# Moving attention work two to three steps sooner inside a feed-forward pipeline, with key-value products further ahead and one copy on another engine

## The chip, the cores and the metric

The kernel runs on one core of one Trainium2 chip. The metric is device microseconds of one execution. A profiled execution also gives a span, which is some 2 us below the time of the same execution. Verdicts use several timed executions of both kernels on the same chip.

## The reference, cut to what matters

Cosine-weighted linear attention over 8 batches of 576 tokens feeds a multiplicative feed-forward block over 4608 tokens:

```python
q_p, k_p = phi(q, cos_w, sin_w), phi(k, cos_w, sin_w)   # relu(x)*cos, relu(x)*sin: 128 features
kv  = einsum('bhsf,bhsd->bhfd', k_p, v)                 # key-value products
num = einsum('bhsf,bhfd->bhsd', q_p, kv)                # numerators
den = einsum('bhsf,bhf->bhs', q_p, sum(k_p)) + 1e-06
x   = num / den                                         # 4608 x 512
out = ((x @ w1) * (x @ w2)) @ w3 @ w_out
```

## The kernel before: the parts that the change and the argument touch

The feed-forward part runs in 9 tiles of 512 tokens. It is a generator that yields after each step, and attention work of later batches is put into the steps by hand. Tile t > 0 starts at step 40+24(t-1); in its first 16 steps it makes a and b products, with one ScalarE copy and one VectorE product for every two steps, and in its last 8 steps the output.

```python
def plan(b, kf, vc, kv, qf, nu, loads=None, xt=None):
    # kf/qf: features of k and q (VectorE half, ScalarE half; q then goes through a DMA transpose to qpT)
    # vc: value copies (GpSimd from batch 2 on); kv: key-value products; nu: numerators; xt: x transposes
    ...
        at(nu[i], lambda c=c: num(b, c))
        at(xt[i] if xt else nu[i], lambda c=c: x_tr(b, c))

def kv_chunk(b, c, i):
    ...                                       # 8 matmuls into pnum
    if i == NCH - 1:                          # after the fifth chunk
        nc.scalar.copy(out=kvs[:, 0:4, :], in_=kvt[:, 0, 0:260])
        nc.vector.tensor_copy(out=kvs[:, 4:8, :], in_=kvt[:, 1, 0:260])

def num(b, c, chain=True):
    nt = ps_att.tile([P, 2, 512], FP32, name="pnum")   # one buffer
    ...                                       # 8 matmuls, then den, reciprocal, xblk on VectorE

def x_tr(b, c, by_vector=False):
    if b >= 2 or (b == 1 and c == 3):
        nc.sync.dma_start_transpose(out=xT[t][:, :, ds(o, R)], in_=xf[rows])
        return
    ...                                       # 4 TensorE transposes into pst
    copy = nc.vector.tensor_copy if by_vector else nc.scalar.copy
    copy(out=xT[t][:, :, ds(o, R)], in_=pst[:, 0:4, rows])
...
bases = [74, 101, 125, 151, 175]              # step of the first numerator of batches 3 to 7
```

In the profiles, kvs is the copy of the key-value products, xblk a normalized block of x, qpT and xT the transposed q features and x, abT the feed-forward product, osb the copied output; pnum, pst and ffnps are PSUM tiles.

## Time and profile before

| | before |
|---|---|
| time, median of 3 (range) | 256.51 us (255.91 to 257.51) |
| time and span of the profiled execution | 258.77 us, 256.8 us |
| TensorE busy | 240.4 us (94%) |
| VectorE, ScalarE, GpSimd busy | 54%, 51%, 37% |
| holes of TensorE past 62 us, each over 0.1 us | 5.5 us |

TensorE's work is fixed, so everything turns on its holes, the stretches in which it stands idle. The profiled execution was itself 2 us slower than the median of the timed ones, which matters later. Its chain of waits, summed by engine (the page's part 4), is a first sign that some holes come from transfers:

```profile
PE 65%; DMA 23%; ACT 5%; issue 2%; DVE 2%; POOL 2%; ACTq 0%; POOLq 0%
```

Past 50 us the same chain, in order of time, has three DMA pieces: the q load of batch 2, the transpose of q at 146.36 that the prediction shows, and an x transpose (columns: start, us, what):

```profile
55.48 9.91 DMA qs<-in_q_dram
...
180.84 5.96 DMA xT<-xblk
```

### The profile page before, as it was taken

The page shows a single profiled execution, that of the slowest core. Times are in us where ns is not written, and L with a number is a line of the kernel's source. Part 1 is how long each engine was busy: PE and PEld are TensorE (multiplying, and loading weights), DVE is VectorE, ACT ScalarE, POOL GpSimd, SP SyncE. Part 2 cuts the span into 40 slices and gives each one's busy share as a digit, 9 for nine tenths or more (in the row PEclk, how much of TensorE's full clock was granted, in tenths as well). Part 3 has the DMA queues.
Part 4 walks back from the last instruction along what each step waited for, and adds up shares of the span by engine and source line. Part 5 has one row for each costly group of instructions (what it writes and reads, how often), then busy time and mean ns, then how long its engine had stood idle before and what let it go on. Part 6 is the DMA issues. An engine that isn't in the chain of part 4 may idle for free.

```text
span 256.8 us, 5008 instructions
## 1 busy us (share of the span) xinstructions
PE 240.4 (94%) x1837; PEld 130.6 (51%) x1867; DVE 138.6 (54%) x330; ACT 130.9 (51%) x270; POOL 94.2 (37%) x197
## 2 busy tenths in 40 slices
PE   8789999999789999999999997899999999999993
PEld 3478554565665445444544453345444544444442
DVE  6775654646668545646566654565567645312320
ACT  2675315667833683466446734474466433433322
POOL 7665140322232344125222711265125108886000
PEclk9999999999999999999999999999999999999999
DMA  6999999799999999999989999999999637998015
GB/s 191 182 194 203 208 205 203 92 127 166 138 157 116 174 155 151 130 127 210 165 119 143 208 118 163 138 178 135 184 151 172 126 72 138 327 289 270 2 39 124
DMA packets 83895, 41.02 MB, mean 160 GB/s; under 512 B 51488, under 2 KB 80416, under 8 KB 83872
## 3 DMA queue, kind: packets, MB, share of 16 engines
q0 software_dynamic: 35456, 27.20, 68.9%
q1 hardware_dynamic: 48256, 13.38, 33.5%
q8 instruction: 14, 0.23, 0.4%
q10 hardware_dynamic: 160, 0.13, 0.2%
q14 instruction: 9, 0.07, 0.1%
HBM read 38.80 MB, written 9.44 MB: 188 GB/s over the span
## 4 chain that ended last, share of the span: by engine, by line
PE 65%; DMA 23%; ACT 5%; issue 2%; DVE 2%; POOL 2%; ACTq 0%; POOLq 0%
PE ffnps L432 37%; PE ffnps L486 18%; DMA qs<-in_q_dram 7%; DMA w3b<-in_moe_w_dram 6%; DMA qpT<-qp 4%; DMA w2b<-in_moe_w_dram 3%; PE pnum L349 3%; PE ffnps L226 3%; DMA xT<-xblk 2%; PE pnum L291 2%; ACT qp L263 2%; DVE kvs L297 1%; PE pst L214 1%; ACT kvs L296 1%; DVE xblk L361 1%
## 5 line engine op out<-in xcount | busy, mean ns | idle before, releaser
L432 PE MATMUL ffnps<-xT,w1b 128*128 128x512 bf16 (+2 forms) x326 | 74.1, 347 | 2.7 <-ACT xT L389 1.1
L432 PE MATMUL ffnps<-xT,w2b 128*128 128x512 bf16 (+2 forms) x329 | 74.6, 348 | 0.4
L473 DVE TENSOR_TENSOR abT<-asb,ffnps 128x512 bf16<-128x512 bf16 x64 | 43.8, 685 | 44.1 <-PE ffnps L432 41.8
L469 ACT CAST asb<-ffnps 128x512 bf16<-128x512 f32 x64 | 37.4, 584 | 55.3 <-PE ffnps L432 48.9
L486 PE MATMUL ffnps<-w34b,abT 128*128 128x512 bf16 x270 | 63.3, 379 | 0.5
L521 POOL COPY seen<-mark 1x1 bf16<-1x1 bf16 x52 | 10.2, 195 | 99.1 <-ACT mark L519 99.1
L432 PEld LDWEIGHTS <-w1b 128*128 128x128 bf16 x336 | 30.7, 98 | 30.2 <-issue 2.8
L432 PEld LDWEIGHTS <-w2b 128*128 128x128 bf16 x336 | 30.3, 98 | 25.7
L486 PEld LDWEIGHTS <-abT 128*128 128x128 bf16 x280 | 26.0, 98 | 27.9 <-DVE abT L473 0.2
L493 ACT COPY osb<-ffnps 128x512 f32<-128x512 f32 x35 | 20.5, 585 | 38.1 <-PE ffnps L486 34.8
L263 ACT ACTIVATE qp<-qs,sinv 128x512 bf16<-128x512 bf16 (+2 forms) x40 | 28.1, 716 | 2.4 <-DMA qs<-in_q_dram 2.4
L361 DVE TENSOR_TENSOR xblk<-pnum,den 128x512 bf16<-128x512 f32 (+1 forms) x39 | 26.9, 691 | 1.4
L263 ACT ACTIVATE kp<-ks,sinv 128x512 bf16<-128x512 bf16 (+1 forms) x35 | 25.0, 720 | 2.3 <-DMA ks<-in_k_dram 2.3
L417 POOL DMA_DIRECT2D out_dram<-osb x42 | 22.2, 534 | 3.8 <-issue 2.8
L283 POOL COPY va<-vs 128x512 bf16<-128x512 bf16 (+1 forms) x30 | 17.7, 624 | 13.3 <-DMA vs<-in_v_dram 11.1
L349 PEld LDWEIGHTS <-qpT 128*128 128x128 bf16 x320 | 15.0, 98 | 12.1 <-issue 4.1
L259 DVE TENSOR_SCALAR qp<-qs,cosv 128x512 bf16<-128x512 bf16 (+1 forms) x40 | 19.2, 491 | 2.7 <-DMA qs<-in_q_dram 2.5
L359 DVE TENSOR_SCALAR den<-pnum 128x8 f32<-128x8 f32 (+1 forms) x39 | 6.4, 164 | 26.0 <-PE pnum L349 25.9
L349 PE MATMUL pnum<-kvs,qpT 128*128 128x65 bf16 x312 | 16.4, 194 | 2.7 <-DMA qpT<-qp 1.4
L226 PE MATMUL ffnps<-woutb,w3T 128*128 128x512 bf16 x62 | 14.8, 379 | 0.1
L291 PEld LDWEIGHTS <-kp 128*128 128x128 bf16 x280 | 11.5, 98 | 5.3 <-PE ffnps L432 1.3
L259 DVE TENSOR_SCALAR kp<-ks,cosv 128x512 bf16<-128x512 bf16 (+1 forms) x35 | 11.7, 343 | 4.1 <-DMA ks<-in_k_dram 4.1
(83 smaller groups left out, 179.9 us busy)
## 6 DMA issues: line engine op xcount, KB each, us to landing
out_dram<-osb POOLq DMA_DIRECT2D x16, 256.0 KB, 4.6
out_dram<-osb POOLq DMA_DIRECT2D x24, 128.0 KB, 3.8
qs<-in_q_dram POOLq DMA_DIRECT2D x9, 256.0 KB, 6.0
ks<-in_k_dram POOLq DMA_DIRECT2D x7, 320.0 KB, 5.8
qs<-in_q_dram POOLq DMA_DIRECT2D x7, 320.0 KB, 6.8
vs<-in_v_dram POOLq DMA_DIRECT2D x7, 320.0 KB, 5.2
ks<-in_k_dram POOLq DMA_DIRECT2D x7, 256.0 KB, 6.6
vs<-in_v_dram POOLq DMA_DIRECT2D x7, 256.0 KB, 5.0
```

Source lines behind the costliest of these rows:

```text
L226: nc.tensor.matmul(acc[:, :], lhsT=w3T[:, lc, :], rhs=woutb[:, lc, :], start=(lc == 0), stop=(lc == 7))
L259: nc.vector.tensor_scalar(out=dst[:R, c, :, 0:D], in0=src[:R, :, c, :], scalar1=0.0, scalar2=cosv[:R, at:at + 1], op0=ALU.max, op1=ALU.mult)
L263: nc.scalar.activation(out=dst[:R, c, 0:n, D:F], in_=src[:R, 0:n, c, :], func=ACTF.Relu, scale=sinv[:R, at:at + 1], bias=0.0)
L283: eng.tensor_copy(out=feat_of(b)[2][:R, c, :, 0:D], in_=raw[b, "v"][:R, :, c, :])
L349: nc.tensor.matmul(nt[:, h // 4, ds((h % 4) * 65, 65)], lhsT=qpT[:, h, ds(at, 128)], rhs=kvs[:, h, :], start=True, stop=True)
L361: nc.vector.tensor_tensor(out=xblk[rows], in0=n4[:, :, :, 0:D], in1=den[rows].unsqueeze(3).to_broadcast([R, 2, 4, D]), op=ALU.mult)
L417: on.dma_start(out=rows[:, :, cols], in_=osb[64 * i:64 * i + rows.shape[0], :, cols])
L432: nc.tensor.matmul(out, lhsT=w[:, kc, ts(jc, 128)], rhs=x[:, kc, tok], start=(kc == 0), stop=(kc == 3))
L469: nc.scalar.copy(out=asb[:], in_=aT[:, :])
L473: nc.vector.tensor_mul(out=abT[:, jc, :], in0=asb[:], in1=bT[:, :])
L486: nc.tensor.matmul(ops[:, :], lhsT=abT[:, jc, ts(ms, 128)], rhs=w34b[:, jc, :], start=(jc == 0), stop=(jc == 7))
L493: nc.scalar.copy(out=osb[:, ms % 2, :], in_=ops[:, :])
```

## The change

The intent is to give the transfers and evictions behind the attention part more steps before TensorE needs them. It has three parts, called (a), (b) and (c) throughout: (a) value copies and key-value products of batches 4 to 7 a step further ahead, (b) batch 1 and 2 around the start of tile 1, (c) the bases, with loads and stores.

```diff
-            at(xt[i] if xt else nu[i], lambda c=c: x_tr(b, c))
+            at(xt[i] if xt else nu[i], lambda c=c: x_tr(b, c, by_vector=(b, c) == (1, 1)))     # (b)
 plan(1, ...
-         ... nu=(35, 37, 38, 40, 43), xt=(37, 38, 40, 42, 43))
+         ... nu=(35, 37, 38, 40, 42), xt=(37, 38, 40, 41, 42))                                  # (b)
 plan(2, ...
-         kv=(45, 46, 46, 47, 47), qf=(40, 41, 42, 43, 44), ...
+         kv=(46, 46, 46, 47, 47), qf=(41, 42, 43, 44, 45), ...                                  # (b)
-    bases = [74, 101, 125, 151, 175]
+    bases = [74, 99, 123, 148, 173]                                                             # (c)
-        plan_loads(b, [last + s for s in (-8, -5, 1, 4, 8, 11)])
+        plan_loads(b, [last + s for s in (-8, -5, 1, 4, 7, 10)])                                # (c)
-             vc=[base + s for s in (-8, -7, -6, -5, -4)],
-             kv=[base + s for s in (-3, -2, -2, -2, -1)],
+             vc=[base + s for s in (-9, -8, -7, -6, -5)],                                       # (a)
+             kv=[base + s for s in (-4, -3, -3, -2, -2)],                                       # (a)
-        at((88, 115, 140, 166)[i] ...
+        at((88, 113, 137, 162)[i] ...                                                           # (c), stores
```

More of the change, by code (lines that the diff above doesn't have):

```diff
@@ L587 @@
     plan(1, kf=(22, 23, 24, 25, 26), vc=(31, 31, 32, 32, 32), kv=(33, 33, 33, 34, 34),
-         qf=(29, 30, 30, 31, 31), nu=(35, 37, 38, 40, 43), xt=(37, 38, 40, 42, 43))
+         qf=(29, 30, 30, 31, 31), nu=(35, 37, 38, 40, 42), xt=(37, 38, 40, 41, 42))
     for c, s in zip(order_of(1), (31, 32, 34)):
@@ L591 @@
     plan_loads(2, (27, 28, 31, 33, 35, 36))
-    plan(2, kf=(33, 35, 37, 39, 40), vc=(41, 42, 43, 44, 45), kv=(45, 46, 46, 47, 47),
-         qf=(40, 41, 42, 43, 44), nu=(48, 50, 52, 54, 57))
+    plan(2, kf=(33, 35, 37, 39, 40), vc=(41, 42, 43, 44, 45), kv=(46, 46, 46, 47, 47),
+         qf=(41, 42, 43, 44, 45), nu=(48, 50, 52, 54, 57))
     plan_loads(3, (46, 49, 53, 55, 58, 61))
@@ L610, in put @@
             store(nc.gpsimd, kept[i][:, :, :], 2 * i, 2)
-        at((88, 115, 140, 166)[i] if i < 4 else 185 + 2 * (i - 4), put)
+        at((88, 113, 137, 162)[i] if i < 4 else 185 + 2 * (i - 4), put)
     g = 0
```

## The prediction

> **What bounds the kernel now.** I read the page's header, engine row and slices first: is one engine busy nearly all the time, and at a full clock?
>
> ```profile
> span 256.8 us, 5008 instructions
> PE 240.4 (94%) x1837; PEld 130.6 (51%) x1867; DVE 138.6 (54%) x330; ACT 130.9 (51%) x270; POOL 94.2 (37%) x197
> PE   8789999999789999999999997899999999999993
> PEclk9999999999999999999999999999999999999999
> ```
>
> TensorE is busy for 240.4 of 256.8 us at full clock; no other engine passes 54%. The change removes no matmul, so it can only fill TensorE's 16.4 us of holes. About 8 us of these are the start (zeros, first k, first q, before 22 us) and the end (the last output copy and store, 4.3 us after the last matmul), which the change does not touch. So I asked for TensorE's own waits:
>
> ```profile
> PE pnum L349 <- DMA qpT<-qp: 1.4, 1, 1.4
> ...
> PE pnum L349 <- DVE kvs L297: 1.2, 4, 0.3
> PE ffnps L432 <- ACT xT L389: 1.1, 1, 1.1
> PE pnum L291 <- DVE xblk L361: 1.0, 1, 1.0
> PE ffnps L432 <- ACT osb L493: 0.8, 1, 0.8
> ```
>
> The columns are total us, times, longest. These five rows sum to 5.5 us (1.36 + 1.20 + 1.12 + 1.04 + 0.80 = 5.52) and are all the holes past 62 us above 0.1 us. They bound what the change can win: 2.1% of the time. The timeline of TensorE places them:
>
> ```profile
> 68.42 1.03 PE L432 MATMUL ffnps<-xT,w1b 128*128 128x256 bf16 x8 [1.12 <-ACT xT L389]
> ...
> 71.37 0.41 PE L291 MATMUL pnum<-va,kp 128*128 128x65 bf16 x8 [1.04 <-DVE xblk L361]
> ...
> 127.20 0.42 PE L349 MATMUL pnum<-kvs,qpT 128*128 128x65 bf16 x8 [0.30 <-DVE kvs L297]
> ...
> 157.07 0.43 PE L349 MATMUL pnum<-kvs,qpT 128*128 128x65 bf16 x8 [1.36 <-DMA qpT<-qp]
> ...
> 162.88 1.02 PE L432 MATMUL ffnps<-xT,w1b 128*128 128x512 bf16 x4 [0.80 <-ACT osb L493]
> ```
>
> Steps to time: tile t of the feed-forward part starts at step 40+24(t-1). Tile 1 (step 40) starts at 62.68 us, tile 5 (136) at 162.88. One step is four matmuls of 512 columns, 0.86 us apart on the timeline; attention work is put in between steps.
>
> The last row's label is wrong. The copy of osb it names is ScalarE's, but tile 5's first matmul needs batch 5's first 192 tokens, and the second of their two transposes was issued on the DMA queue at 156.72 and took 6.1 us to land, that is at 162.8, right before 162.88. It is a late DMA, not a PSUM buffer.
>
> **What the Trainium skill says.** "PSUM — Partial Sum Buffer", section "Engine vs sequencer instructions": the ScalarE, VectorE and GpSimd queues are strict FIFO, and matmuls start in program order. So one late input stops all work behind it; the trace agrees (a 1.12 us hole for one 0.57 us copy). "VectorE: DVE Perf Modes", section on the TRN2 errata: a copy out of PSUM costs ScalarE 172 + columns cycles at 1.2 GHz, 570 ns for 512 columns, and VectorE 120 + columns/2 at 0.96 GHz in a doubled mode, 392 ns. The trace has 580 and 425 ns for the x copy, so I use these. "DMA: Bandwidth & Descriptors", section "Issuing engines are not separate DMA queues": transfers from all engines run on the same 16 DMA engines and interleave. The trace agrees: the transposes of q for batch 5 beside a 512 KB store and two loads of k took a median of 9.0 us and at most 10.7, those of batch 7 with less beside them 3.2.
>
> **The change part by part.**
>
> (a) Key-value products a step further ahead, batches 4 to 7. Now the last of five chunks stands at base-1 and the first numerator at base. Between them TensorE has one step, 0.86 us, while two evictions in a row must finish (ScalarE 376 ns, VectorE 429 ns), with ScalarE first ending an asb copy. Around 125 to 127 us the last product ends at about 126.0, ScalarE starts kvs at 126.30, VectorE ends at 127.15, the numerator starts at 127.20. At base-2 there is a second step of 0.86 us, more than the hole of 0.30. I take all four: -1.2 us. Value copies also move one step, so the GpSimd copies stay ahead.
>
> (b) Batch 1 into tile 1. Tile 1's second half needs x of chunk 2, copied by ScalarE behind several activations:
>
> ```profile
> 67.18 0.72 ACT L263 ACTIVATE qp<-qs,sinv 128x512 bf16<-128x512 bf16 x1
> ...
> 67.81 0.57 ACT L389 COPY xT<-pst 128x512 bf16<-128x512 bf16 x1
> ```
>
> The change gives ScalarE one copy less (580 ns at 63.99), moves this transpose from step 42 to 41, the q features of batch 2 one step later, and batch 1's last numerator from 43 to 42. The instruction order confirms it: ScalarE now has kp (64 rows), asb, then xT. But there is a price. VectorE's 425 ns copy goes ahead of chunk 2's normalization:
>
> ```profile
> 64.24 0.17 DVE L359 TENSOR_SCALAR den<-pnum 128x8 f32<-128x8 f32 x1 [0.83 <-PE pnum L349]
> 64.44 0.20 DVE L360 RECIPROCAL den<-den 128x8 f32<-128x8 f32 x1
> 64.68 0.69 DVE L361 TENSOR_TENSOR xblk<-pnum,den 128x512 bf16<-128x512 f32 x1
> ```
>
> The copy runs 63.99 to 64.42, den starts about 64.45 instead of 64.24, xblk ends about 65.58 instead of 65.37. TensorE comes to that transpose at 64.91 now, not 65.78, and waits until about 65.63: a new hole of 0.7 us. Then xT is ready at about 66.6, while the second half is reached two half-tile groups later, near 67.9: the 1.12 hole goes. Batch 2's products move from 45 to 46 and the numerator before them from 43 to 42, four steps apart in place of two, so their wait for xblk (1.04) goes too. Sum: -1.12 - 1.04 + 0.72 = -1.44 us.
>
> (c) Batches 4 to 7 sooner. Numerators run at base, base+2, and so on; bases 101, 125, 151, 175 become 99, 123, 148, 173. Tile 5 starts at step 136, so batch 5's second transpose has 11 steps (125 to 136) in place of 9 (127 to 136): 1.73 us more for a landing 0.8 us late. -0.8 us.
>
> (d) The wait at 157.07 is not addressed as such. The chain has its cause:
>
> ```profile
> 146.36 10.67 DMA qpT<-qp
> ```
>
> This transpose belongs to q features at base-6 and serves the numerator at base+5; the distance is 11 steps before and after, the loads of the next batch keep base-8 and base-5, and the store keeps base-10. So if the transfers pile up likewise, 1.36 us stays; if that was a chance of this execution, it goes. I take half: -0.7 us.
>
> Sum: -1.2 - 1.44 - 0.8 - 0.7 = -4.1 us at the profile. I give back 0.3 for new small waits and 0.5 since the three timed runs (255.91 to 257.51) need not have every DMA delay of the profiled one, so there may be less to win. 256.5 - 3.3 = 253.2 us, 1.3% less.
>
> **The rivals.** First, v arrives too late. For batch 4 the load's second half moves from 85 to 84 but its first product from 98 to 95, 13 steps down to 11; batch 5 keeps 10, batch 6 goes from 12 to 11, batch 7 from 10 to 11. Loads of v land in about 5 us, 6 steps, and the copies take 0.62 us each. Batch 7 lived with 10 steps without a hole, so I give a new wait 15%; it would be about 1 us per batch, 255 to 256 us in all.
>
> Second, VectorE becomes the bound: with numerators at 99, 101 and 123, 125 more of them fall in a tile's first 16 steps, where two steps (1.73 us) hold a product (0.69), a normalization (1.1) and q features (0.35 to 0.5), 2.1 to 2.3 us. Against: batch 4 had this already at 101 and 103, and TensorE had no hole at 129. Four PSUM buffers take up a lag of two steps. If it binds, 0.5 us a batch: 254.5 us.
>
> Third, the DMA pile-up moves instead of going: the wait of 1.36 us may come again in batch 5, 6 (transposes already took 7.0 us median there) or both: 254 to 255 us.
>
> Fourth, everything goes and (d) too, without the hole of (b): 251.0 to 251.5 us, the best case.
>
> **Range and chances.** Between (a) + half of (b), about 254.8, and all of it less the new hole, 251.7: the range is 252.0 to 255.0. Faster by over 2% means below 251.4, practically all 5.5 us: 6%. Slower by 2% needs 5 us of new waits, which no view suggests: 1%. Within 2%: 93%.
>
> **What would show it.** (a) No row of TensorE waiting for kvs, from four. (b) The hole before the first-half-to-second-half matmul and the one before batch 2's products gone, and one of about 0.7 us before an x transpose near 65.6. (c) No hole at tile 5's start. (d) Either the qpT row gone or still 1 to 1.5 us. PE busy stays at 240 us. The prediction is wrong if GpSimd's value copies or late loads appear as TensorE's releasers, if DMA rows grow over 2 us, or if the timed kernel keeps its time while these rows vanish from the profile: then the profile's holes were not the timed runs' holes.

## The result, and the profile after

| | before | changed |
|---|---|---|
| time, median of 4 (range) | 256.81 us (255.91 to 257.51) | 254.26 us (253.35 to 259.06) |
| ratio of fast runs (95% interval) | | 0.989 (0.984 to 0.994) |
| span of the profiled execution | 256.8 us | 251.3 us |

Ratios here and below are the mean time of one kernel's fast runs over that of the other's of the same rounds, so not quite the ratio of the medians. The changed kernel's run of 259.06 us was slow (clock 0.989) and is left out of the ratio. The change makes the kernel 1.1% faster, an interval that excludes no change but stays under the 2% at which these verdicts say faster; the prediction was 253.2 us, 1.3%.

The page of the changed kernel (span, busy time of each engine, TensorE's busy tenths in 40 slices, and the chain by engine):

```profile
span 251.3 us, 5013 instructions
PE 240.8 (96%) x1838; PEld 130.7 (52%) x1867; DVE 139.0 (55%) x331; ACT 130.5 (52%) x269; POOL 94.3 (38%) x197
PE   8889999999999999999999999999999999999993
...
PE 77%; DMA 13%; DVE 4%; issue 2%; POOL 1%; ACT 1%; ACTq 0%; POOLq 0%; DVEq 0%
```

TensorE is busy as long as before (240.8 us), so what was won is holes. The three 7s in its slices are gone, the chain's DMA share falls from 23% to 13%, and it has no DMA piece at all past 50 us. TensorE's own waits (total us, times, longest) beside the five rows that the prediction shows:

```profile
PE pst L387 <- DVE xblk L361: 1.1, 3, 0.4
...
PE pnum L349 <- DVE xblk L361: 0.3, 1, 0.3
```

All five rows of before are gone: past 62 us there is no wait over 0.1 us for kvs, for xT, for osb (which was a late DMA), for qpT or before batch 2's products. Two rows stand for what was put in their place. The first had two waits of 0.36 and 0.35 us before and now has a third, at the moved x transpose of batch 1; the second is new. On TensorE's timeline:

```profile
65.06 0.40 PE L387 MATMUL pst<-identb,xblk 128*128 128x128 bf16 x4 [0.42 <-DVE xblk L361]
...
125.10 0.42 PE L349 MATMUL pnum<-kvs,qpT 128*128 128x65 bf16 x8 [0.25 <-DVE xblk L361]
```

There are two more holes like the last one, 0.14 us each, at the second numerators of batches 5 and 7. They are visible on VectorE's timeline ahead of 125.10:

```profile
122.97 0.69 DVE L473 TENSOR_TENSOR abT<-asb,ffnps 128x512 bf16<-128x512 bf16 x1 [0.96 <-PE ffnps L432]
123.57 0.34 DVE L259 TENSOR_SCALAR qp<-qs,cosv 64x512 bf16<-64x512 bf16 x1
123.84 0.15 DVE L359 TENSOR_SCALAR den<-pnum 128x8 f32<-128x8 f32 x1
124.02 0.20 DVE L360 RECIPROCAL den<-den 128x8 f32<-128x8 f32 x1
124.26 0.69 DVE L361 TENSOR_TENSOR xblk<-pnum,den 128x512 bf16<-128x512 f32 x1
```

The first numerator of batch 4 runs at 122.70 now, with no wait. VectorE first does a feed-forward product and the last q features, and only then normalizes. The second numerator needs the single pnum buffer that this normalization frees, at 124.95.

The two profiles differ by 5.5 us of span, twice what the timed runs show. One pair of executions is not enough to say where the typical 2.6 us came from.

### The profile page after: what moved, and what is told of

It is laid out like the page before. It is cut to its first block, busy times and chain, and to the rows that moved or that the text cites. A ratio compares the mean times of both kernels' runs of the same rounds, so it can differ in the third digit from the quotient of the medians.

```text
span 251.3 us, 5013 instructions
## 1 busy us (share of the span) xinstructions
PE 240.8 (96%) x1838; PEld 130.7 (52%) x1867; DVE 139.0 (55%) x331; ACT 130.5 (52%) x269; POOL 94.3 (38%) x197
## 4 chain that ended last, share of the span: by engine, by line
PE 77%; DMA 13%; DVE 4%; issue 2%; POOL 1%; ACT 1%; ACTq 0%; POOLq 0%; DVEq 0%
PE ffnps L432 41%; PE ffnps L486 24%; DMA w3b<-in_moe_w_dram 6%; PE pnum L349 4%; PE pnum L291 4%; PE ffnps L226 3%; DMA w2b<-in_moe_w_dram 3%; DMA qs<-in_q_dram 3%; DVE xblk L361 2%; DVE abT L473 1%; PE pst L214 1%; PE pst L322 1%; DVE den L360 1%; PE pst L387 0%; DVE qp L259 0%
```

## The experiments

Twelve runs were made, of eleven different kernels, on several chips. Kernels are compared only within the same rounds.

### The kernel before once more

No edit. Is every hole of the first profile a property of the kernel?

> The kernel before, unchanged, profiled once more. Theory T1 (mine): the DMA rows of the first profile (1.36 us at the wait for qpT in batch 5, 0.80 us at the start of tile 5) are a chance of that execution, whose own time, 258.8 us, was 2 us above the median; then at least one of the two rows is gone or under half here, while the four waits for kvs (0.30 each), the 1.12 us for xT and the 1.04 us before batch 2's products are all here again to 0.1 us. Rival T2: both DMA rows belong to the schedule and come back at 1 to 1.5 and 0.5 to 1 us. Ratio 1.00 either way.

Measured: 257.23 us, ratio 0.999 (0.993 to 1.005); the span of this profile is 254.8 us. TensorE's waits:

```profile
PE ffnps L432 <- ACT xT L389: 1.6, 1, 1.6
...
PE pnum L349 <- DVE kvs L297: 1.2, 4, 0.3
PE pnum L291 <- DVE xblk L361: 1.0, 1, 1.0
```

The waits for kvs and for batch 2's products come back to the hundredth. The waits of 1.36 us (qpT) and 0.80 us (start of tile 5) are both absent, so the first profile had 2 us that this one has not, which is about the difference of the two spans. The wait for xT is 1.59 us, not 1.12, so it too depends on something that varies.

### Part (b) alone

The (b) lines of the diff, on the kernel before.

> Only the batch 1 and 2 part: x copy of chunk 1 by VectorE, last numerator and two transposes a step sooner, batch 2's products and q features a step later. T1: the two holes of 2.16 us between 65 and 72 us become one of 0.4 us, minus 1.7 us: ratio 0.993. T2 (most of the gain is from the sooner batches 4 to 7): this part is lost again in later waits, ratio 0.997 or more. The kvs waits stay at four times 0.30 us.

Measured: 257.18 us, ratio 0.995 (0.989 to 1.001). The ratio lies between T1's 0.993 and T2's 0.997. Between 65 and 72 us a single hole of 0.42 us is left, as expected, but on TensorE's timeline two later tiles wait:

```profile
161.20 1.02 PE L432 MATMUL ffnps<-xT,w1b 128*128 128x512 bf16 x4 [2.25 <-ACT kp L263]
...
185.60 0.60 PE L432 MATMUL ffnps<-xT,w1b 128*128 128x512 bf16 x2 [0.50 <-ACT mark L519]
```

These are the starts of tiles 5 and 6. Both labels are wrong again. Asked for the landing of the x transposes issued there (154.5 and 155.9 us), the trace gives:

```profile
DMA to landing us min/median/max: 5.7/6.1/6.6
```

The one issued at 154.5 lands after 6.6 us, at 161.1, and TensorE starts at 161.20. The Trainium skill, "Perfetto Trace Analysis", section "DMA Instruction — HWDGE (DVE, Sync)", says that the profiler's window of such an instruction does not contain the engines' data movement. This trace agrees: the row shows 1.2 us, and the landing comes 5.7 to 6.6 us after the issue. So a timeline alone doesn't show this dependency; the landing has to be asked for. A wait of 0.35 us for batch 2's transposes of q is new here as well; it returns below. The late landing that the first profile showed was not a single accident, then, and my theory T1 was wrong to call it one.

### Part (a) alone

```diff
-             vc=[base + s for s in (-8, -7, -6, -5, -4)],
-             kv=[base + s for s in (-3, -2, -2, -2, -1)],
+             vc=[base + s for s in (-9, -8, -7, -6, -5)],
+             kv=[base + s for s in (-4, -3, -3, -2, -2)],
```

> Only the value copies and key-value products of batches 4 to 7 a step sooner, at the old bases. T1: the four waits for kvs go and no new wait comes, since the numerators stay where they were (the 0.25 and 0.14 us waits for xblk in the changed kernel come from numerators in a tile's first 16 steps): minus 1.2 us, ratio 0.995. Rival: the wait before the first numerator only moves to the second one, minus 0.5 us or less, ratio 0.998, with rows waiting for xblk.

Measured: 255.58 us, ratio 0.990 (0.985 to 0.996). The profile decides what the timing can't. From its TensorE waits:

```profile
PE ffnps L432 <- DMA xT<-xblk: 0.7, 1, 0.7
PE pnum L349 <- DVE xblk L361: 0.5, 2, 0.3
```

No wait for kvs is left, and there are waits for xblk at all four second numerators: 0.25, 0.15, 0.25 and 0.15 us (the view's row lists two). So 1.2 us of one wait became 0.8 us of another, at the old bases. The rival was nearly right, and my reason for these waits (numerators in a tile's first 16 steps) fell. What the timelines offer in its place is argued, not tested alone: in the kernel before, VectorE starts the product that stands ahead of the normalization at 150.80 us, while TensorE still waits for kvs to start batch 5's first numerator at 150.94. In the changed kernel the first numerator of batch 4 starts at 122.70 and the product at 122.97. The pause of TensorE had given VectorE a lead. A start of tile 6 with a late x transpose (0.71 us) is here too. The ratio of 0.990 is more than 0.4 us, and I do not claim the rest for this part: in this profile q of batch 2 happened to land early and the wait for xT was 0.10 us.

### Part (c) alone

The (c) lines of the diff, on the kernel before.

> Only the bases 99, 123, 148, 173 with loads and stores that follow them, products still ending a step before the numerators. T1: nothing to win in a typical run, since the late DMA is a chance; the kvs waits stay and VectorE's lag adds some tenths: ratio 0.998 to 1.002. T2: the sooner batches are the main gain, minus 1.5 to 2 us in every run: ratio 0.992 to 0.994.

Measured: 256.39 us, ratio 0.994 (0.989 to 0.999). From its TensorE waits:

```profile
PE ffnps L432 <- ACT xT L389: 1.2, 1, 1.2
...
PE pnum L291 <- DVE xblk L361: 1.0, 1, 1.0
PE pnum L349 <- DVE kvs L297: 0.9, 3, 0.3
```

The holes of (a) and (b) are here, but for batch 6, whose wait for kvs is 0.07 us at the new bases; there is none at the start of tiles 4 to 6. T1 had expected nothing to win; T2's figure is nearer. From here on I hold T3: the starts of tiles 5 and 6 are late in most executions with the old bases.

### The changed kernel once more

No edit.

> The changed kernel, unchanged, profiled once more. The waits of a fixed order (0.36 and 0.42 us before x transposes of batch 1, 0.1 to 0.25 us for xblk at the second numerators) come back to 0.1 us. Theory T3, formed after the first runs: with the old bases the x transposes of batches 5 and 6 land within 0.1 us of, or after, the tile that needs them (waits of 0 to 2.3 us in four profiles), with the new ones 0.1 to 1.1 us ahead; then no wait over 0.3 us at the starts of tiles 4 to 6 here. Rival: the first profile of the changed kernel was a lucky one and a wait of 0.5 us or more stands at one of these starts. Ratio 0.988 to 0.991.

Measured: 254.85 us (253.80 to 255.75), ratio 0.989 (0.984 to 0.993). The fixed waits come back to 0.01 us: 0.36, 0.42, and 0.25, 0.15, 0.15 us at second numerators. No wait stands at a tile's start, where x had landed 3.0, 0.7 and 1.6 us earlier (tiles 4, 5, 6). New are three waits of 0.66 us in all for GpSimd's value copies of batch 2, whose v load landed late.

### The q features of batch 2 alone

```diff
-         qf=(40, 41, 42, 43, 44), nu=(48, 50, 52, 54, 57))
+         qf=(41, 42, 43, 44, 45), nu=(48, 50, 52, 54, 57))
```

> The kernel before with the q features of batch 2 a step later, nothing else. If the wait of 1.1 to 1.6 us at tile 1's second half comes from ScalarE standing before its first q activation until q of batch 2 has landed, with the x copy behind it, this edit alone takes it below 0.3 us, with ScalarE's copy of chunk 1 still in place; the 1.04 us before batch 2's products stays. Rival: ScalarE's extra copy is the cause, and 0.5 us or more is left. At the starts of tiles 5 and 6, old bases: a wait of 0.3 us or more at one of them is likely (three of four profiles so far).

One look: 258.24 us, state unknown. From its TensorE waits:

```profile
PE ffnps L432 <- ACT kp L263: 1.9, 1, 1.9
PE pnum L291 <- POOL va L283: 1.5, 1, 1.5
```

The wait for xT is gone without any help from VectorE. ScalarE's timeline has the cause, first in the kernel before, then here:

```profile
65.48 0.72 ACT L263 ACTIVATE qp<-qs,sinv 128x512 bf16<-128x512 bf16 x1 [0.91 <-DMA qs<-in_q_dram]
...
65.87 0.72 ACT L263 ACTIVATE qp<-qs,sinv 128x512 bf16<-128x512 bf16 x1
```

In the kernel before, the load of q landed at 65.39 us and ScalarE stood 0.91 us for it; here it landed at 65.79, no sooner, and ScalarE stood for nothing, since other work now fills that time. So it was not an early load that removed the wait. The mechanism is shown: ScalarE's strict queue stood at a q activation until the load of q had landed, and the copy that TensorE needed was behind it. Once the wait goes, the next late thing shows: 1.5 us for the value copies, whose v load lands after q. The start of tile 5 is late by 1.93 us, again under a ScalarE label.

### Part (a) taken back from the changed kernel

```diff
-             kv=[base + s for s in (-4, -3, -3, -2, -2)],
+             kv=[base + s for s in (-3, -2, -2, -2, -1)],
```

(and vc likewise)

> The changed kernel with value copies and products of batches 4 to 7 put back by a step. If the step ahead trades a wait for kvs against a smaller one for xblk (as it did at the old bases, 1.2 for 0.8 us), then the waits for kvs of 0.30 us are here again, three or four, and the waits for xblk at the second numerators (0.53 us in all) are gone. Rival: the waits for xblk come from the new bases and stay.

One look: 255.34 us, state unknown. The waits for kvs are back, on TensorE's timeline for batch 5:

```profile
148.47 0.42 PE L349 MATMUL pnum<-kvs,qpT 128*128 128x65 bf16 x8 [0.30 <-DVE kvs L297]
```

Batch 7 has 0.30 us as well and batch 6 0.07; at batch 4 a late q transpose (1.61 us) hides it. No wait for xblk is left. So the two waits trade, at the new bases as at the old: at most 0.96 us (three times 0.30 and 0.07, as with (c) alone) against 0.54 us. Of the three or four waits of 0.30 us that I expected, two are here.

### The last q features a step sooner

```diff
-             qf=[base + s for s in (-12, -9, -6, -3, 0)],
+             qf=[base + s for s in (-12, -9, -6, -3, -1)],
```

> The changed kernel with the last q features of batches 4 to 7 at base-1 in place of base. VectorE then does them (0.34 us) ahead of the product that stands before the first normalization, so xblk is ready 0.3 us sooner and the waits for xblk at the second numerators (0.25, 0.14, 0.14) go below 0.1 each: minus 0.5 us, ratio to the kernel before 0.002 below that of the changed kernel, too little for the timing alone. Rival: VectorE's backlog is the product itself, and the waits stay.

> The version with the last q features at base-1, once more, for a second sample of its time and a profile in the fast state. No wait for xblk at the second numerators, and ratio 0.985 to 0.988, if its better ratio in the last call was more than chance; 0.988 to 0.990 if it was chance.

The first run: 254.72 us, ratio 0.985 (0.980 to 0.991), its profile slow by its time and so not used. But its clock is 0.999 and TensorE waits 4.2 us for q transposes in it; the rule that leaves it and a second of the six runs out by their time may leave out late transfers, and then the ratio flatters. The second: 253.18 us (252.04 to 253.84), ratio 0.981 (0.976 to 0.986). Its VectorE timeline at batch 4:

```profile
123.20 0.33 DVE L259 TENSOR_SCALAR qp<-qs,cosv 64x512 bf16<-64x512 bf16 x1
124.24 0.69 DVE L473 TENSOR_TENSOR abT<-asb,ffnps 128x512 bf16<-128x512 bf16 x1 [0.71 <-PE ffnps L432]
124.85 0.16 DVE L359 TENSOR_SCALAR den<-pnum 128x8 f32<-128x8 f32 x1
```

The features now stand ahead of the product, and no wait for xblk over 0.1 us is left at the second numerators. The mechanism is shown. This version is faster than the kernel before by 1.5 to 1.9%; that it beats the changed kernel is not shown: on one chip, the ratios were 0.985 and 0.989 and their intervals overlap.

### Parts (a) and (b) without the bases

> Everything of the change except the sooner bases (bases, loads and stores of batches 4 to 7 as before). T3: holes filled ahead of tiles 5 and 6 are taken back at their starts, since the x transposes of batches 5 and 6 land no sooner for it: waits at the starts of tiles 5 and 6 sum to 1.5 to 3 us (2.75 in the run with part b alone), ratio to the kernel before 0.994 to 0.998. Rival: the three parts add up and the bases are worth a third, ratio 0.990 to 0.993, with less than 0.8 us at those starts.

Measured: 255.96 us (253.72 to 258.83), ratio 0.990 (0.984 to 0.996). The profile fell on its fastest run, 253.72 us, and has no wait at the starts of tiles 5 and 6; x had landed 0.84 and 0.05 us ahead. My expectation missed for this execution, so the late landing is not forced by filling the holes ahead of it, and the ratio is the rival's. The timing can't divide the gain either: the parts alone sum to 2.1% (1.0, 0.5 and 0.6), the whole has 1.1%, and each is uncertain by some 0.5%. What the six profiles with the old bases, in the fast or unknown state, do show is that the late landing depends on the execution (waits at the two starts together):

| old bases | us | new bases | us |
|---|---|---|---|
| before | 0.87 | (c) alone | 0 |
| before again | 0.07 | changed | 0 |
| (b) alone | 2.75 | changed again | 0 |
| (a) alone | 0.71 | (a) taken back | 0 |
| q features of batch 2 | 2.25 | copy on ScalarE | 0 |
| (a) and (b) | 0 | later q features (again) | 0 |

The mean is 1.1 us with the old bases (6.65 / 6), nothing over 0.06 us with the new.

### The x copy back on ScalarE

```diff
-            at(xt[i] if xt else nu[i], lambda c=c: x_tr(b, c, by_vector=(b, c) == (1, 1)))
+            at(xt[i] if xt else nu[i], lambda c=c: x_tr(b, c))
```

> The changed kernel with the x copy of batch 1's chunk 1 back on ScalarE. If VectorE's copy only delays the normalization of chunk 2, the 0.42 us wait before the next x transpose shrinks to 0.1 to 0.3 us and nothing new comes, since ScalarE is not late once the q features stand behind the copy of chunk 2: ratio as the changed kernel, 0.988 to 0.990. Rival: ScalarE is late again and a wait for xT of 0.3 us or more stands before tile 1's second half.

Measured: 253.81 us, ratio 0.984 (0.980 to 0.989). On TensorE's timeline:

```profile
64.96 0.40 PE L387 MATMUL pst<-identb,xblk 128*128 128x128 bf16 x4 [0.35 <-DVE xblk L361]
```

No wait for xT comes back, and this hole is 0.35 us in place of 0.42. VectorE's copy is not what removed the wait; it costs 0.07 us here.

### Three edits together

The q features at base-1, the copy on ScalarE, and batch 2's numerators at (48, 51, 53, 55, 57) in place of (48, 50, 52, 54, 57).

> The changed kernel with three edits: last q features of batches 4 to 7 at base-1, the x copy of chunk 1 back on ScalarE, batch 2's second to fourth numerators a step later (51, 53, 55). If a step later for batch 2's q features is what made its second numerator wait for its DMA transpose (0.2 to 1.0 us, once 3.2 us, in five of the eight runs that have it), the later numerators end that wait; no wait for xblk at the second numerators of batches 4 to 7; ratio 0.980 to 0.984. Rival: the later numerators only push the wait on, or their x transposes come late at tile 2, ratio 0.985 or more.

Measured: 253.98 us, ratio 0.989 (0.984 to 0.994). From TensorE's timeline:

```profile
81.62 0.43 PE L349 MATMUL pnum<-kvs,qpT 128*128 128x65 bf16 x8 [1.48 <-DMA qpT<-qp]
```

The rival held: the wait for batch 2's transposes of q moved to another numerator. Waits of 0.2 to 1.5 us for these transposes stand in five of nine profiles, in the fast or unknown state, of kernels with the later q features of batch 2, and in none of the four with the early ones; the mean over the nine is 0.36 us. That is a cost of part (b) which the prediction did not have.

## Why the prediction was right or wrong

The time, 254.26 us against 253.2, is inside the range, and the ratio of 0.989 against 0.987. By its steps, with two profiles of each kernel (TensorE's holes past 62 us, in us):

| step | before, twice | changed, twice | predicted gain | measured gain, mean |
|---|---|---|---|---|
| (a) kvs, then xblk | 1.20, 1.20 | 0.53, 0.55 | 1.2 | 0.66 |
| (b) xT, x transpose, batch 2's products | 2.16, 2.63 | 0.42, 1.08 | 1.44 | 1.65 |
| (c) starts of tiles 5 and 6 | 0.87, 0.07 | 0, 0 | 0.8 | 0.47 (1.1 over all old-base profiles) |
| (d) qpT in batch 5 | 1.36, 0 | 0, 0 | 0.7 | 0.68 |

These sum to 3.5 us. The two timed comparisons of the changed kernel gave 2.6 and 3.0 us between medians, so holes before 62 us and the scatter of single executions are in the rest.

The first profile of before was of an execution slower than most, and a mean over more profiles is fairer. My estimate, from all profiles in the fast or unknown state that fit: (a) 0.66 us; (b) 2.04 (four profiles without this part) less 0.82 (six with all of it), 1.2 us; (c) 1.1 us; (d) 1.36 us over the six with the old bases, 1.61 us over the seven with the new ones, 0.23 us each, so nothing. These sum to 3.0 us, nearer to the timed 2.6 and 3.0.

That the forecast of 3.3 us comes near is partly luck: the parts were forecast at 4.1 us, too much in (a) and (d) and too little in (c), and the 0.8 us given back for other reasons made up for it. One sum of the range is off too: (a) and half of (b) leave 254.6 us, not about 254.8; nothing rests on it.

**Bounds and place of the gain: right.** TensorE's busy time stayed at 240 to 241 us and the time moved by its holes. The reading that the osb label hid a late DMA was confirmed by two more profiles with other wrong labels on the same wait.

**(a): the term "all four" was mis-sized.** The waits for kvs did go, but a wait for xblk took the place of about half: 0.66 us won in place of 1.2. Of these, 0.4 us came at the old bases; the rest needs the new ones, at which batch 6 has neither wait over 0.1 us. The second rival had named the engine; it sized the wait at 0.5 us a batch (0.14 to 0.25 measured) and put it down to the new bases, which the run of (a) alone refuted.

**(b): right as a sum, for partly wrong reasons.** The new hole was 0.42 us and not 0.72. I let TensorE arrive at 64.91, the start of its next matmul in the old timeline, where the matmul ahead of it ends only at 65.07 (64.04 + 1.03); and the transpose started at 65.06, or 65.50 on the old timeline, whose tile 1 starts 0.44 us later, where I had said 65.63. I put the late x copy down to several activations ahead of it and credited ScalarE's lighter load; the runs show that ScalarE stood 0.91 us for the load of q, that the later q features ended this, and that the copy on VectorE was not needed. Not foreseen were the two waits that follow: for the v load and for the q transposes of batch 2. GpSimd's value copies as releasers were my own sign of being wrong, and in one of the two profiles of the changed kernel they appear.

**(c): right in direction.** The slack given, two steps or 1.73 us, was enough in every profile with the new bases. The size is a mean over executions that scatter from 0 to 2.75 us, not the 0.8 us of one profile.

**(d): right that it was partly a chance, lucky in the size.** The second profile of before had neither DMA row. That the table's 0.68 us meets my half is the luck of two profiles: the wait of 1.61 us with (a) taken back is a pile-up that moved, as the third rival had it, if to batch 4 and not to 5 or 6, and no run here shows that the change made it rarer. What remains open is why the same transfer (the last q transpose of batch 5) lands after 9.0 us in one profile of the kernel before and after 5.1 us in the other; no run here tells.

## What to carry to other kernels

When an engine that is nearly full waits on strict queues, look at what stands ahead of the awaited instruction in its engine's queue; here batch 2's q activations, moved by a step, removed over 1 us, and one moved q feature removed the wait that had replaced another. Before crediting a hole's whole length, ask what the other engines did in that pause: they may have been catching up, and then a part of it comes back elsewhere. Profile the kernel before twice, since a hole that comes from a transfer's landing can be 0 or 1.4 us in the same kernel, and schedule such work by the slowest landing, not by the one that was seen.

## What the Trainium skill lacked or had wrong

- "DMA: Bandwidth & Descriptors", section "Latency and other measured facts", gives a DMA transpose a bandwidth (261 GB/s) and no latency beside other traffic. The first profile shows 3.1 to 3.4 us from issue to landing with little beside it (most transposes of q of batch 7) and up to 10.7 us beside loads and a store; for a tile of 256 KB that bandwidth alone would be an estimated 1 us.
- No page says how far the landing of the same transfer varies between executions of one kernel. The x transpose that tile 5 needs took 4.4 us in one profile of the kernel before and 6.1 us in the other.
- "VectorE: DVE Perf Modes", the section on the TRN2 errata, is near but low for these sizes: ScalarE's copy out of PSUM of 512 columns took 580 ns against 570 by its formula, of 260 columns 376 against 360; VectorE's took 425 ns against 392, and 429 against 396.
- "Perfetto Trace Analysis" does not warn that a wait can be put down to another engine where a DMA ends it. The same wait at the start of tile 5 was labelled osb of ScalarE in one profile and kp of ScalarE in two others; only the landing of the x transpose showed the cause.
